# A recurrence and two MoE layers on one core: preparing chunks further ahead, solving two triangular systems together, and spreading the recurrence's steps between the MoE blocks

## The chip, the cores and the metric

The kernel runs on one core of one Trainium2 chip. The metric is the device time of one execution in microseconds (us). Engines are called as in the profile: PE is TensorE (matmuls), PEld its weight loads, DVE is VectorE, ACT is ScalarE, POOL is GpSimd, and SP is the engine that issues the DMAs here. A median over three runs is given, and one execution was recorded by the hardware profiler.

## What is computed

The reference is a recurrence over 768 time steps for 4 batches of 8 heads with a 40 by 40 state each, then a dense two-layer block (MoE1), then a mixture of 8 experts with dense gates (MoE2):

```python
# recurrence, for each t:  y_t = r_t S;  S <- S * w_t - (S a_t) b_t^T + v_t k_t^T
for t in range(S):
    y[:, :, t] = np.einsum('bhd,bhde->bhe', rt, state)
    Sa = np.einsum('bhde,bhe->bhd', state, at)
    state = state * wt[:, :, None, :] - np.einsum('bhd,bhe->bhde', Sa, bt) + np.einsum('bhd,bhe->bhde', vt, kt)
# MoE1, 3072 tokens, 320 -> 2048 -> 320
h = x @ w_in;  x = np.where(h > 0, h, np.exp(np.minimum(h, 0)) - 1) @ w_out
# MoE2: gates P normalised over rows and columns 8 times, then
for e in range(8):
    out += P[:, e:e + 1] * (np.maximum(x @ w1[e], 0) @ w2[e])     # 320 -> 1024 -> 320
```

## The kernel before

**Chunks.** The 768 steps are cut into 24 chunks of 32. Within a chunk the recurrence becomes matrix products and a triangular solve; from chunk to chunk the state Y is handed on. The work of one chunk c is cut into steps, each a small Python function:

- `ld` (lines 263 to 269) issues the DMAs of WA and KE; `lu` that of VU; `lv` those of rB and rO. WA, KE, xE, F and rO have one buffer each, VU three.
- `prep` (283 to 308) runs two scans on DVE (F, line 292, and xE, line 297) and element work on POOL (KE, line 306; aE, 299; WA, 307) and ACT. It needs WA and KE, and it ends with aE, its copy aB, and a scaled KE.
- `E3` (349) multiplies KE and aB on PE (line 338), masks the product on DVE into Am (line 342), writes Am to DRAM (Ad, line 357) and reads it back in another layout as LT (line 359). `E1` (313) and `E2` (322) transpose KE and xE on PE (lines 318, 328). `E4` multiplies Am by VU on PE (line 367).
- `T` is the solve (`tsolve_`, 370): a work tile Wk is loaded with a constant by DMA (line 374), then 31 rounds of two DVE instructions follow, a product (line 379, into Tt) and a subtraction (line 386, in Wk), each of which needs the one before it; Wk goes to DRAM (Td, line 390, four DMAs) and back as TT (line 394, four DMAs).
- `H1` (405; PE line 416) needs the state; `H2` (417; PE line 425) multiplies by TT; `H3` (435; PE line 446, DVE line 456) makes the new state Y; `H4` (458; PE line 465) transposes it into Ss.
- `O1` (473; PE line 479), `O2` (484; PE line 338, mask Gm on DVE line 342) and `O3` (488; PE lines 497 and 502, DVE line 504) make the chunk's output, which goes to DRAM as yd (line 509).

The recurrence proper is the ring H1, H2, H3 and H1 of the next chunk; E, T and prep of a chunk don't depend on the state and can be done ahead.

**MoE1.** Its 3072 tokens are 12 blocks of 256, two chunks each. A block begins with `xprep` (513): it reads two tiles yt (one buffer, line 520), transposes each on PE (line 523) into X by ACT (526) and DVE (527, 528). Then 16 units follow. A unit has two halves of eight 256-column matmuls: `m1_mm1` (534; PE line 538; g on DVE line 543, gh on ACT 545, gl on POOL 547) and, two units later, `m1_mm2` (552; PE lines 561 to 565), which reads gh and gl.

**What sets the order.** Instructions are traced in the order of the string PLAN["order"] (line 26), once per chunk: `m+2` stands for two halves of MoE1, `E3+2` for E3 of the chunk two ahead, `O1+-1` for O1 of the chunk before. On PE this order is kept literally in the loop (`pin`, line 115). On the other engines a list scheduler takes, by its own model of time, what is ready first, with the traced position as the priority (T and the MoE1 halves are put 300 places back, prep 300 forward, line 30); what it fixes is then the order in which the engine runs, strictly one after the other. PLAN["start"] (27) is a longer list for the first two chunks, in which MoE1's weights are also converted (`w`, 64-bit floats to pairs of 32-bit ones, with raw tiles from the pool cv, line 153). After the recurrence the rest of MoE1 and then MoE2 (lines 648 to 780) run on PE without a break.

Of the kernel before, what the change touches and what calls it, by code (L numbers as in the profile page):

```python
# [9 lines left out]
F32 = mybir.dt.float32  # L10
# [12 lines left out]
PLAN = {  # L23
# [74 lines left out]
def build(ctx, tc, r, k, v, w, a, b, w_in, w_out, wg, w1, w2, wa_d, kb_d, re_d, ro_d, vt_d, wp_d, consts, out, C, off):  # L98
    nc = tc.nc
# [50 lines left out]
    pa_p = moe.enter_context(tc.tile_pool(name="pa_p", bufs=1, space=PSUM))  # L150
    r1 = rec.enter_context(tc.tile_pool(name="r1", bufs=1, side="right"))
    r2 = rec.enter_context(tc.tile_pool(name="r2", bufs=2, side="right"))
    cv = cvx.enter_context(tc.tile_pool(name="cv", bufs=3, side="right"))
    rp = rec.enter_context(tc.tile_pool(name="rp", bufs=1, space=PSUM, side="right"))

    Wt = mw.tile([128, 5, DFF], F32R, name="Wt")
# [65 lines left out]
    first = {}  # L222
    Y = r1.tile([128, NG, B, D], F32, name="Y")
    Ss = r1.tile([128, NG, 2, 2, D], F32, name="Ss")
    TTs = [r1.tile([128, H, 64], F32, name=f"TT{i}") for i in range(3)]
    wr = r1.tile([128, 4 * NG, C + 1], F32, name="wr")
    wq = r1.tile([128, 4 * NG, C], F32, name="wq")
    dr = r1.tile([128, 4 * NG, C + 1], F32, name="dr")
    dq = r1.tile([128, 4 * NG, C], F32, name="dq")
    Yw = r1.tile([128, NG, B, 64], F32, name="Yw")  # L230
    Ywv = Yw[:, :, :, 0:D]
    Ams = [r1.tile([128, 2, H, 64], F32, name=f"Am{i}") for i in range(2)]
    Gm = r1.tile([128, 2, H, 64], F32, name="Gm")
    aB = r1.tile([128, NG, 2, 2, 64], F32, name="aB")
    rB = r1.tile([128, NG, 2, 2, 64], F32, name="rB")
    wmm = per.tile([128, NCH], F32, name="wmm")
    CI = C // 4

    work = {None: (wr, wq, dq, aB)}

    def rec_init():
        for t in (wr, wq, dr, dq):
            V.memset(t, 0.0)
        work[1] = (early(1, "wr", [4 * NG, C + 1]), early(1, "wq", [4 * NG, C]), early(1, "dq", [4 * NG, C]), early(1, "aB", [NG * 2 * 2, 64]).rearrange("p (g u j) t -> p g u j t", u=2, j=2))
        for t in work[1]:
# [37 lines left out]
    def prep(c):  # L283
        z = st[c]
        NX = 4 * NG
        wr, wq, dq, z.aB = work.get(c, work[None])
        wf = z.WA[0:HR, 0].rearrange("p g t -> p (g t)")
        wv = wf.rearrange("p (x t) -> p x t", x=NX)
        V.tensor_scalar(out=wr[0:HR, :, 1:C + 1], in0=wv[:, :, ::-1], scalar1=WLO, scalar2=WHI, op0=ALU.max, op1=ALU.min)
        V.tensor_scalar(out=wq[0:HR, :, 1:C], in0=wv[:, :, 0:C - 1], scalar1=WLO, scalar2=WHI, op0=ALU.max, op1=ALU.min)  # L290
        F = early(c, "F", [NX, C + 1])
        V.tensor_tensor_scan(out=flat(F)[0:HR], data0=flat(wr)[0:HR], data1=flat(dr)[0:HR], initial=0.0, op0=ALU.mult, op1=ALU.add)  # L292
        z.Wf = r2.tile([128, NX], F32, tag="Wf", name="Wf", bufs=3)
        G.tensor_copy(out=z.Wf[0:HR], in_=F[0:HR, :, C])
# [12 lines left out]
        G.tensor_tensor(out=wv, in0=wv, in1=wr[0:HR, :, 1:C + 1][:, :, ::-1], op=ALU.subtract)
        A.activation(out=wf, in_=wf, func=AF.Square, accum_out=wmm[0:HR, c:c + 1])
# [61 lines left out]
    def tsolve_(c):  # L370
        z = st[c]
        Wk = r2.tile([128, CI, C], F32, tag="Wk", name="Wk")
        tmp = r2.tile([128, CI * (C - 1)], F32, tag="Tt", name="Tt")
        SY.dma_start(out=Wk.rearrange("p i t -> p (i t)"), in_=consts[:, nidk:nidk + CI * C])
        for j in range(C - 1):
            ni = j // 4 + 1
            nt = C - 1 - j
# [13 lines left out]
        z.TT = TTs[c % 3]  # L391
# [93 lines left out]
        z = st[c]  # L485
        yield from masked(banks("O2", c)[0], 2 * D, lambda u, g: z.uE[:, u, g, :], rB, Gm)

    def O3(c):
        z = st[c]
        PO = banks("O3", c)  # L490
        x = z.xT
        y = x if c else mt.tile([128, 384], F32, tag="yt", name="yt", bufs=1)
        for j in range(2):
            if c > 0:
                for g in range(NG):
                    for bb in range(B):
                        pin(T.matmul(PO[j][C * bb:C * bb + C, D * g:D * g + D], lhsT=z.rO[64 * (bb % 2):64 * (bb % 2) + D, bb // 2, j, g, :], rhs=Ss[64 * (bb % 2):64 * (bb % 2) + D, g, bb // 2, j, :], start=(g == 0), stop=False, skip_group_check=True))
                        yield
# [446 lines left out]
    with ExitStack():  # L945
        loads(0)
        loads(1)
        SY.dma_start(out=cst, in_=consts[:, 0:ncst])
        SY.dma_start(out=wgs[:, 0:2, :], in_=wg[0:256, :].rearrange("(k p) e -> p k e", p=128))
        SY.dma_start(out=wgs[0:64, 2, :], in_=wg[256:320, :])  # L950

# [84 lines left out]
        for c in range(2, NCH + 1):  # L1036
            for n, o in order:
# [53 lines left out]
```

## Time and profile before

| | |
|---|---|
| median of 3 runs | 2436.05 us (2433.66 to 2437.01) |
| the profiled execution | 2433.81 us, its span 2431.9 us |
| PE busy | 2185.4 us, 90% of the span |
| PE weight loads | 1991.4 us, 82% |
| DVE | 1127.6 us, 46% |
| ACT | 731.1 us, 30% |
| POOL | 503.8 us, 21% |
| chain that ended last | PE 67%, DVE 19%, DMA 8% |

The profiled execution is 2.2 us below the median. Busy time of PE is what the profile models from the starts of pipelined matmuls; idle time "before" a group of instructions is that of its engine, with what ended it. Granted clock is the share of full speed (2.4 GHz) that TensorE had on average in a stretch; its other level is half of that, 1.2 GHz.

### The profile page before, as it was taken

To read this page: it belongs to the slowest core of one execution; us is meant where nothing else is said; L and a number is where in the kernel's file an instruction comes from. 1 tells how busy PE (TensorE), PEld (TensorE's weight loads), DVE (VectorE), ACT (ScalarE), POOL (GpSimd) and SP (SyncE) were. 2 spreads that over 40 slices of the span, in tenths; PEclk is the share of its full clock that TensorE was granted. 3 is DMA by queue.
4 is the path that set the end of the run, shared out by engine and by line. 5 is a ranking of instruction groups with operands and counts; after the bars stand their busy time and mean duration, and the time that the engine had idled before them with its cause. 6 is when DMAs were issued, how large, how long until landed. Compare 5 with 4: busy or idle time off the path is not lost.

```text
span 2431.9 us, 47949 instructions
## 1 busy us (share of the span) xinstructions
PE 2185.4 (90%) x19908; PEld 1991.4 (82%) x19908; DVE 1127.6 (46%) x2878; ACT 731.1 (30%) x1627; POOL 503.8 (21%) x570
## 2 busy tenths in 40 slices
PE   2557887888888889999999999999999999999998
PEld 2456776787877788889999999999999999999998
DVE  7898677777877764253222222222222222222222
ACT  2343443444444444532311211211211212212111
POOL 6353333333333322500200200200200101101000
PEclk9998898988899989999999999999999999999999
DMA  5342323333233321420100100100100100000000
GB/s 153 109 143 75 99 72 85 82 84 91 76 94 80 86 75 37 116 58 1 45 4 1 48 1 1 48 1 1 48 1 7 42 1 22 27 1 19 12 22 34
DMA packets 171771, 121.67 MB, mean 50 GB/s; under 512 B 103000, under 2 KB 151512, under 8 KB 171544
## 3 DMA queue, kind: packets, MB, share of 16 engines
q1 hardware_dynamic: 171544, 118.52, 17.9%
q8 instruction: 158, 2.59, 0.5%
q14 instruction: 69, 0.57, 0.1%
HBM read 99.99 MB, written 18.48 MB: 49 GB/s over the span
## 4 chain that ended last, share of the span: by engine, by line
PE 67%; DVE 19%; DMA 8%; issue 2%; SPq 2%; POOL 1%; ACT 1%; DVEq 0%; ACTq 0%; POOLq 0%
PE h L704 29%; PE pa L746 9%; PE pa L745 9%; PE pa L744 9%; DVE Wk L386 5%; DVE Tt L379 5%; PE ph L538 3%; DMA WA<-in_wa 2%; DMA LT<-Ad 1%; DVE g L543 1%; DMA yt<-yd 1%; DVE F L292 1%; DVE Gm L342 1%; DVE Am L342 1%; PE a L561 1%
## 5 line engine op out<-in xcount | busy, mean ns | idle before, releaser
L704 PE MATMUL h<-X,a 128*128 128x512 f32 x3072 | 774.8, 394 | 0.0
L708 DVE SCALAR_TENSOR_TENSOR hl<-h,hh 128x512 fp32r<-128x512 f32 x384 | 264.8, 690 | 879.7 <-ACT hh L707 879.4
L704 PEld LDWEIGHTS h<-X,a 128*128 128x128 f32 x3072 | 564.2, 188 | 102.9
L707 ACT ACTIVATE hh<-h 128x512 fp32r<-128x512 f32 x384 | 230.2, 600 | 1019.5 <-PE h L704 1015.9
L745 PE MATMUL pa<-a,hl 128*128 128x320 f32 x1536 | 474.5, 309 | 0.0
L744 PE MATMUL pa<-a,hh 128*128 128x320 f32 x1536 | 472.3, 309 | 1.1 <-ACT acc L751 0.9
L746 PE MATMUL pa<-a,hh 128*128 128x320 f32 x1536 | 468.7, 310 | 0.0
L745 PEld LDWEIGHTS pa<-a,hl 128*128 128x128 f32 x1536 | 288.8, 188 | 15.9
L744 PEld LDWEIGHTS pa<-a,hh 128*128 128x128 f32 x1536 | 288.8, 188 | 15.9 <-ACT acc L751 1.3
L746 PEld LDWEIGHTS pa<-a,hh 128*128 128x128 f32 x1536 | 287.3, 188 | 0.1
L672 POOL TENSOR_TENSOR a<-rw,a 128x384 fp32r<-128x384 f32 x64 | 65.6, 1025 | 1057.9 <-ACT a L670 1055.2
L538 PE MATMUL ph<-X,Wt 128*128 128x256 f32 x1536 | 252.2, 311 | 5.2 <-DVE g L543 5.1
L379 DVE TENSOR_TENSOR Tt<-Wk,LT 128x60 f32<-128x60 f32 (+24 forms) x744 | 209.0, 284 | 88.4 <-DMA LT<-Ad 59.2
L547 POOL TENSOR_TENSOR gl<-g,gh 128x256 fp32r<-128x256 f32 x192 | 159.1, 830 | 389.2 <-ACT gh L545 280.3
L538 PEld LDWEIGHTS ph<-X,Wt 128*128 128x128 f32 x1536 | 216.6, 209 | 14.3 <-DVE g L543 8.5
L386 DVE TENSOR_TENSOR Wk<-Wk,Tt 128x60 f32<-128x60 f32 (+24 forms) x744 | 215.2, 292 | 17.9
L545 ACT ACTIVATE gh<-g 128x256 fp32r<-128x256 f32 x192 | 80.0, 417 | 232.6 <-DVE g L543 190.0
L755 DVE SCALAR_TENSOR_TENSOR acc<-pa,Pg,acc 128x320 f32<-128x320 f32 x168 | 84.3, 544 | 114.8 <-PE pa L746 114.8
L543 DVE SCALAR_TENSOR_TENSOR g<-m,ph 128x256 f32<-128x256 f32 x192 | 79.9, 416 | 104.1 <-ACT m L541 95.3
L540 ACT ACTIVATE m<-ph 128x256 f32<-128x256 f32 x192 | 73.2, 381 | 89.7 <-PE ph L538 88.1
L541 ACT ACTIVATE m<-m 128x256 f32<-128x256 f32 x192 | 79.8, 416 | 4.7
L425 PE MATMUL P<-RH,TT 64*64 64x40 f32 x768 | 33.7, 248 | 48.7 <-DMA TT<-Td 47.1
(173 smaller groups left out, 2412.7 us busy)
## 6 DMA issues: line engine op xcount, KB each, us to landing
LT<-Ad SPq DMA_DIRECT2D x24, 512.0 KB
rw<-in_moe_w SPq DMA_DIRECT2D x64, 160.0 KB
WA<-in_wa SPq DMA_DIRECT2D x24, 416.0 KB
KE<-in_kb SPq DMA_DIRECT2D x24, 416.0 KB
rw<-in_moe_w SPq DMA_DIRECT2D x64, 128.0 KB
VU<-in_vt SPq DMA_DIRECT2D x24, 320.0 KB
raw<-in_wp SPq DMA_DIRECT2D x16, 384.0 KB
raw<-in_moe_w_out SPq DMA_DIRECT2D x16, 320.0 KB
```

The costliest lines, as they stand in the source:

```text
L379: V.tensor_tensor(out=tv, in0=Wk[:, 0:ni, j:j + 1].to_broadcast([128, ni, nt]), in1=z.LT[:, j, j + 1:C].unsqueeze(1).to_broadcast([128, ni ...
L386: dve["T"] = V.tensor_tensor(out=Wk[:, 0:ni, j + 1:C], in0=Wk[:, 0:ni, j + 1:C], in1=tv, op=ALU.subtract)
L538: pin(T.matmul(ph, lhsT=Wt[0:kp, wi, 128 * f:128 * f + 128], rhs=X[0:kp, xi, :], start=(i == 0), stop=(i == 7)))
L543: V.scalar_tensor_tensor(out=g, in0=m, scalar=-1.0, in1=ph, op0=ALU.add, op1=ALU.max)
L547: G.tensor_tensor(out=gl, in0=g, in1=gh.bitcast(F32), op=ALU.subtract)
L704: T.matmul(h, lhsT=a1[:, wi, :], rhs=X[bk][:, xi, :], start=(i == 0), stop=(i == 7))
L707: A.activation(out=hh, in_=h, func=AF.Relu)
L708: V.scalar_tensor_tensor(out=hl, in0=h, scalar=0.0, in1=hh.bitcast(F32), op0=ALU.max, op1=ALU.subtract)
L744: T.matmul(o, lhsT=hh[:, ts_], rhs=a2[:, 0, :], start=(f == 0), stop=False)
L745: T.matmul(o, lhsT=hl[:, ts_], rhs=a2[:, 0, :], start=False, stop=False)
L746: T.matmul(o, lhsT=hh[:, ts_], rhs=a2[:, 1, :], start=False, stop=(f == NF2 - 1))
L755: V.scalar_tensor_tensor(out=at, in0=o, scalar=Pg[:, tt, e:e + 1], in1=at, op0=ALU.mult, op1=ALU.add)
```

## The change

The loop's order and the start list are new, O3 is cut in two, T is called for two chunks at once, and buffers are added so that a chunk can be prepared three ahead (E3, E2, E1 for c+3; ld and prep for c+4, where it was E for c+2, prep for c+2 and ld for c+3). Wk is filled on POOL from a tile idk that is loaded once. To make room, cv has two buffers instead of three and a scratch area for DMA descriptors is smaller. The number of MoE1 halves per chunk (16 in the string) stays.

```diff
-    "order": "E4 H1 m+2 O1+-1 H2 m+3 O2+-1 H3 m+3 ld+3 lu+1 prep+2 O3+-1 m+2 H4 E3+2 T+2 m+2 E1+2 m+2 x E2+2 m+2 lv w",
+    "order": "E4 m+1 O2+-1 m+1 H1 x m+1 O3a+-1 m+1 lv H2 m+1 O3b+-1 m+2 H3 m+1 E3+3 m+2 H4 m+1 E2+3 m+1 E1+3 ld+4 lu+1 m+2 O1 prep+4 T+3 m+2 w",
     "start": ... O3_0 becomes O3a_0 O3b_0, O3_1 becomes O3a_1 O3b_1, and at its end
+     ... prep_4 E3_4 E2_4 E1_4 ld_5 prep_5
-    cv = cvx.enter_context(tc.tile_pool(name="cv", bufs=3, side="right"))
+    cv = cvx.enter_context(tc.tile_pool(name="cv", bufs=2, side="right"))
-    TTs = [... for i in range(3)]        # z.TT = TTs[c % 3]
+    TTs = [... for i in range(4)]        # z.TT = TTs[c % 4]
-    Ams = [... for i in range(2)]        # z.Am = Ams[c % 2]
+    Ams = [... for i in range(3)]        # z.Am = Ams[c % 3]
+    idk = r1.tile([128, CI * C], F32, name="idk")
     # Wf, KB, xT: 3 -> 4 buffers; aE: 2 -> 4
 def tsolve_(c):
-        SY.dma_start(out=Wk.rearrange("p i t -> p (i t)"), in_=consts[:, nidk:nidk + CI * C])
+        G.tensor_copy(out=Wk.rearrange("p i t -> p (i t)"), in_=idk)
-    def O3(c):
+    def O3a(c):       # the products of Ss and rO (line 497), for both j
+        if c == 0:
+            return
+    def O3b(c):       # the products of Gm and KB (line 502), the multiplication by xT, the store
     # in try_xprep
-            if ... and ("O3", 2 * xp + 1) in done:
+            if ... and ("O3b", 2 * xp + 1) in done:
     # in the loop over c
+                elif n == "T":
+                    if (c + o) % 2 and c + o < NCH:
+                        with tc.high_priority(offset=PLAN["po"]["T"]):
+                            tsolve(c + o - 1, c + o)
-    nc = bacc.Bacc("TRN2", target_bir_lowering=False, num_devices=1)
+    nc = bacc.Bacc("TRN2", target_bir_lowering=False, num_devices=1, dynamic_dma_scratch_size=4096)
```

`tsolve(c1, c2)` was there already, for the start list: it takes the rounds of the two solves alternately.

## Rows read from the trace of the kernel before

**Rows 1.** Busy time of the engines, granted clock and DMA in four stretches: start, steady recurrence, the rest of MoE1, MoE2.

```profile
core 0: us, PE busy (x) PEld busy (x) DVE busy (x) ACT busy (x) POOL busy (x), PEclk, DMA share, GB/s
0.00:250.00 250.00, 127.12 (x1945) 111.37 (x1945) 215.53 (x613) 87.46 (x205) 117.93 (x143) 0.94 0.43 120
250.00:950.00 700.00, 589.84 (x9449) 548.55 (x9450) 510.54 (x1551) 298.53 (x771) 240.79 (x265) 0.90 0.31 81
950.00:1100.00 150.00, 142.97 (x1168) 133.75 (x1167) 57.13 (x130) 72.70 (x164) 44.68 (x56) 0.98 0.27 78
1100.00:2431.00 1331.00, 1325.46 (x7349) 1197.70 (x7348) 344.45 (x584) 272.45 (x488) 100.43 (x106) 1.00 0.06 18
```

**Rows 2.** PE's waits in the steady stretch, 250 to 950 us: who waited for whom, us in total, times, the longest; and one group of PE instructions there, H4, which has 8 matmuls a chunk.

```profile
PE P L523 <- DMA yt<-yd: 40.2, 8, 5.7
PE a L562 <- POOL gl L547: 25.6, 8, 6.1
PE P L318 <- DVE Am L342: 16.3, 8, 2.1
PE P L523 <- DVE Tt L379: 8.6, 2, 4.8
PE P L338 <- DVE xT L504: 8.1, 7, 1.3
PE P L497 <- DVE Gm L342: 3.4, 7, 0.6
...
L465 PE MATMUL P<-cst,Yw 104*128 104x104 f32 x144 | 16.5, 259 | 0.0
```

**Rows 3.** DVE in the same stretch: the two instructions of the solve (busy, mean ns | idle before them), and DVE's waits.

```profile
L386 DVE TENSOR_TENSOR Wk<-Wk,Tt 128x60 f32<-128x60 f32 (+24 forms) x558 | 163.3, 293 | 15.3
L379 DVE TENSOR_TENSOR Tt<-Wk,LT 128x60 f32<-128x60 f32 (+24 forms) x558 | 160.5, 288 | 84.4 <-DMA LT<-Ad 59.2 <-DMA Wk<-in_consts 8.3 <-DMA Td<-Wk 2.0
...
DVE Tt L379 <- DMA LT<-Ad: 59.2, 14, 8.3
DVE g L543 <- ACT m L541: 50.0, 40, 4.8
DVE Am L342 <- PE P L338: 15.9, 9, 2.6
```

**Rows 4.** PE at full clock, from the timeline (start us, us, engine, line): H3, H1 and a half of MoE1.

```profile
655.74 1.30 PE L446 MATMUL P<-VU,KB 64*40 64x40 f32 x64
...
679.78 0.79 PE L416 MATMUL P<-Yw,aE 40*32 40x40 f32 x64
680.50 1.22 PE L538 MATMUL ph<-X,Wt 128*128 128x256 f32 x8
```

**Rows 5.** From the timeline (start us, us, engine, line): after an E1 the KE of the next chunk is fetched, POOL waits for it, and gl and a half of MoE1 behind it.

```profile
673.70 0.88 PE L318 MATMUL P<-cst,KE 104*128 104x104 f32 x8
...
675.63 0.43 SPq L269 DMA_DIRECT2D KE<-in_kb  x1
...
678.81 0.42 DVE L543 SCALAR_TENSOR_TENSOR g<-m,ph 128x256 f32<-128x256 f32 x1 [0.68 <-ACT m L541]
...
679.92 2.34 POOL L306 TENSOR_TENSOR KE<-KE,F 104x512 f32<-104x512 f32 x2 [4.10 <-DMA KE<-in_kb]
...
682.22 1.42 POOL L547 TENSOR_TENSOR gl<-g,gh 128x256 fp32r<-128x256 f32 x2
...
683.00 0.39 PE L562 MATMUL a<-gl,WoA 128*128 128x256 f32 x1 [1.15 <-POOL gl L547]
```

**Rows 6.** The timeline of one xprep: transposes of its first tile, the load of the second, its transposes, X; and a half of MoE1 just after it.

```profile
711.59 0.49 PE L523 MATMUL P<-cst,yt 128*128 128x128 f32 x3
...
713.64 0.60 SPq L520 DMA_DIRECT2D yt<-yd  x1
...
717.23 0.88 PE L523 MATMUL P<-cst,yt 128*128 128x128 f32 x3 [5.15 <-DMA yt<-yd]
...
718.14 0.49 ACT L526 ACTIVATE X<-P 128x384 fp32r<-128x384 f32 x1 [5.22 <-PE P L523]
718.49 2.06 PE L538 MATMUL ph<-X,Wt 128*128 128x256 f32 x8
...
719.97 0.40 DVE L527 TENSOR_TENSOR X<-P,X 128x256 fp32r<-128x256 f32 x1
720.29 0.28 DVE L528 TENSOR_TENSOR X<-P,X 128x128 fp32r<-128x128 f32 x1
```

**Rows 7.** DVE in the start list, where two solves run alternately (x2: two instructions together), and just after, where one of them has ended.

```profile
71.40 0.34 DVE L379 TENSOR_TENSOR Tt<-Wk,LT 128x28 f32<-128x28 f32 x2
71.66 0.34 DVE L386 TENSOR_TENSOR Wk<-Wk,Tt 128x28 f32<-128x28 f32 x2
71.92 0.34 DVE L379 TENSOR_TENSOR Tt<-Wk,LT 128x24 f32<-128x24 f32 x2
...
74.08 0.21 DVE L379 TENSOR_TENSOR Tt<-Wk,LT 128x48 f32<-128x48 f32 x1
74.32 0.21 DVE L386 TENSOR_TENSOR Wk<-Wk,Tt 128x48 f32<-128x48 f32 x1
74.56 0.21 DVE L379 TENSOR_TENSOR Tt<-Wk,LT 128x49 f32<-128x49 f32 x1
```

**Rows 8.** One solve from its first instruction to its last, its way to DRAM and back, and the H2 that needs it.

```profile
639.48 1.03 DVE L379 TENSOR_TENSOR Tt<-Wk,LT 128x31 f32<-128x31 f32 x1 [3.53 <-DMA LT<-Ad]
...
667.05 0.17 DVE L386 TENSOR_TENSOR Wk<-Wk,Tt 128x8 f32<-128x8 f32 x1
...
667.25 1.23 SPq L390 DMA_DIRECT2D Td<-Wk  x2
...
677.41 0.59 SPq L394 DMA_DIRECT2D TT<-Td  x1
...
684.90 0.31 PE L425 MATMUL P<-RH,TT 64*64 64x40 f32 x4
```

**Rows 9.** PE's longest wait in the start, 80 to 260 us.

```profile
PE P L425 <- DMA TT<-Td: 47.1, 8, 16.1
```

**Rows 10.** POOL: a copy of 64 columns and the difference gl of 256 (columns as on the page; the first from its line's own view: duration ns min/median/max).

```profile
L505 POOL COPY xT<-xT x23: 236/237/238, 130.9 to 980.2; 128x64 f32<-128x64 f32 x23
...
L547 POOL TENSOR_TENSOR gl<-g,gh 128x256 fp32r<-128x256 f32 x192 | 159.1, 830 | 389.2 <-ACT gh L545 280.3
```

More of the change, by code (lines that the diff above doesn't have):

```diff
@@ L224, in build @@
     Ss = r1.tile([128, NG, 2, 2, D], F32, name="Ss")
-    TTs = [r1.tile([128, H, 64], F32, name=f"TT{i}") for i in range(3)]
+    TTs = [r1.tile([128, H, 64], F32, name=f"TT{i}") for i in range(4)]
     wr = r1.tile([128, 4 * NG, C + 1], F32, name="wr")
@@ L231, in build @@
     Ywv = Yw[:, :, :, 0:D]
-    Ams = [r1.tile([128, 2, H, 64], F32, name=f"Am{i}") for i in range(2)]
+    Ams = [r1.tile([128, 2, H, 64], F32, name=f"Am{i}") for i in range(3)]
     Gm = r1.tile([128, 2, H, 64], F32, name="Gm")
@@ L249, in rec_init @@
             V.memset(bank[i], 0.0)
-        for t in (aB, wmm, rB, Ams[0], Ams[1], *TTs, Yw, Gm):
+        for t in (aB, wmm, rB, *Ams, *TTs, Yw, Gm):
             G.memset(t, 0.0)
@@ L292, in prep @@
         V.tensor_tensor_scan(out=flat(F)[0:HR], data0=flat(wr)[0:HR], data1=flat(dr)[0:HR], initial=0.0, op0=ALU.mult, op1=ALU.add)
-        z.Wf = r2.tile([128, NX], F32, tag="Wf", name="Wf", bufs=3)
+        z.Wf = r2.tile([128, NX], F32, tag="Wf", name="Wf", bufs=4)
         G.tensor_copy(out=z.Wf[0:HR], in_=F[0:HR, :, C])
@@ L297, in prep @@
         V.tensor_tensor_scan(out=flat(z.xE)[0:HR], data0=flat(wq)[0:HR], data1=flat(dq)[0:HR], initial=0.0, op0=ALU.mult, op1=ALU.add)
-        z.aE = r2.tile([128, NG, B * C], F32, tag="aE", name="aE")
+        z.aE = r2.tile([128, NG, B * C], F32, tag="aE", name="aE", bufs=4)
         G.tensor_tensor(out=z.aE[0:HR].rearrange("p g t -> p (g t)"), in0=z.WA[0:HR, 1].rearrange("p g t -> p (g t)"), in1=flat(z.xE)[0:HR], op=ALU.mult)
@@ L314, in E1 @@
         z = st[c]
-        z.KB = r2.tile([128, 2, H * D], F32, tag="KB", name="KB", bufs=3)
+        z.KB = r2.tile([128, 2, H * D], F32, tag="KB", name="KB", bufs=4)
         for u in range(2):
@@ L324, in E2 @@
         z = st[c]
-        z.xT = r2.tile([128, 384], F32, tag="xT", name="xT", bufs=3)
+        z.xT = r2.tile([128, 384], F32, tag="xT", name="xT", bufs=4)
         xv = z.xE.rearrange("p (g b) t -> p g (b t)", g=NG)
@@ L350, in E3 @@
         z = st[c]
-        z.Am = Ams[c % 2]
+        z.Am = Ams[c % 3]
         yield from masked(PS["E3"][0], HR, lambda u, g: z.KE[:, g, u, :], z.aB, z.Am)
@@ L390, in tsolve_ @@
             SY.dma_start(out=Td.rearrange("x (i q) t -> q x i t", q=4)[q], in_=Wk[q::4])
-        z.TT = TTs[c % 3]
+        z.TT = TTs[c % 4]
         for bb in range(B):
@@ L486, in O2 @@
         yield from masked(banks("O2", c)[0], 2 * D, lambda u, g: z.uE[:, u, g, :], rB, Gm)
-    def O3(c):
+    def O3a(c):
+        z = st[c]
+        PO = banks("O3", c)
+        if c == 0:
+            return
+        for j in range(2):
+            for g in range(NG):
+                for bb in range(B):
+                    pin(T.matmul(PO[j][C * bb:C * bb + C, D * g:D * g + D], lhsT=z.rO[64 * (bb % 2):64 * (bb % 2) + D, bb // 2, j, g, :], rhs=Ss[64 * (bb % 2):64 * (bb % 2) + D, g, bb // 2, j, :], start=(g == 0), stop=False, skip_group_check=True))
+                    yield
+    def O3b(c):
         z = st[c]
@@ L493, in O3 @@
         for j in range(2):
[L494 to L498, printed above, removed]
             for g in range(NG):
@@ L948, in build @@
         SY.dma_start(out=cst, in_=consts[:, 0:ncst])
+        SY.dma_start(out=idk, in_=consts[:, nidk:nidk + CI * C])
         SY.dma_start(out=wgs[:, 0:2, :], in_=wg[0:256, :].rearrange("(k p) e -> p k e", p=128))
@@ L958, in try_xprep @@
             xp = ms["xp"]
-            if (late or xp == 0) and xp < NB1 and xp <= bk + 1 and ("O3", 2 * xp + 1) in done:
+            if (late or xp == 0) and xp < NB1 and xp <= bk + 1 and ("O3b", 2 * xp + 1) in done:
                 xprep(xp)
@@ L990, in build @@
             wgen += wi_[k0 + i:k0 + i + 1] + wo_[i:i + 1]
-        fns = dict(ld=loads, lu=loadv, lv=loads2, prep=prep, H1=H1, H2=H2, H3=H3, H4=H4, E1=E1, E2=E2, E3=E3, E4=E4, T=tsolve, O1=O1, O2=O2, O3=O3,)
+        fns = dict(ld=loads, lu=loadv, lv=loads2, prep=prep, H1=H1, H2=H2, H3=H3, H4=H4, E1=E1, E2=E2, E3=E3, E4=E4, T=tsolve, O1=O1, O2=O2, O3a=O3a, O3b=O3b)
         done = {("ld", 0), ("ld", 1)}
```

2 rows, old and new, of the table PLAN are left out of this document.

## The prediction

> **What bounds the kernel now.** I read first the busy time by stretches. From 1100 us on PE is busy for all but 5.5 of 1331 us at full clock, and DVE, ACT and POOL have little to do: MoE2 is bound by PE, and the change doesn't touch it [rows 1]. The reader is to see in the same view that the stretch from 250 to 950 us is different: PE is busy for 590 of 700 us, at a granted clock of 0.90, so 110 us are idle and about 20% of the time (140 us) is at 1.2 GHz. Since PE's order is written out and all its work is the same before and after, the end moves by as much as idle time and half-clock time of PE change, wherever in the recurrence that is.
>
> 18 chunks pass in that stretch (144 transposes of H4, 8 a chunk [rows 2]), so a chunk takes 38.9 us. The second view is PE's waits there [rows 2]. Six waits make nearly all of the idle time: xprep's load of yt, 40.2 and 8.6 us (the second line names DVE's solve, but it stands before the same transposes, so I count it to yt: 48.8 us in 10 cases); gl from POOL, 25.6; E1 behind the mask of E3, 16.3; E3 behind the output's multiplication by xT, 8.1; O3 behind the mask Gm, 3.4. The third view is DVE [rows 1, 3]: it is busy for 510.5 us, of which the solve has 163.3 + 160.5 = 324, or 18.0 us a chunk, and it stands for 59.2 us before LT has landed.
>
> **Neighbours in PE's order.** Two waits come from steps that stand too near to each other. Before, E3 is followed by two halves of MoE1 and then E1, which overwrites a bank that E3's mask is still read from; O3 is followed by two halves and H4, and then E3, on a bank that O3's result is still read from. After, E3 and E1 have four halves, H4 and E2 between them; O3b and E3 three halves and H3. A half takes 1.22 us [rows 4], and these waits are at most 2.1 us long [rows 2], so one or two more halves are enough: 16.3 + 8.1, **minus 24 us** (0 at worst).
>
> A third pair comes nearer. The mask Gm is read from O2's bank, which O3's first products overwrite. Before, H3 and three halves stand between; after, H1 and two halves, 1.30 - 0.79 + 1.22 = 1.7 us less [rows 4]. In 7 of 18 chunks PE waited there already, 0.5 us each [rows 2]; x lies between in every second chunk after the change and hides it. That leaves 9 chunks: where it waited (3 or 4) 2.2 us, in the others something like 0.4, 10 us, against 3.4 before: **plus 7 us**, bounds -3 and 17.
>
> **gl.** KE has one buffer: when E1 (673.70) has read it, SP fetches the next at 675.63, POOL stands at KE's scaling until 679.92, takes 2.34 us for it, and only then makes two gl, while PE waits for the first until 683.00, 9.3 us after that E1 [rows 5]. After the change ld stands right behind E1 as well, so POOL will wait as long. But what PE does meanwhile is more: two halves, O1, two halves, E4, a half, O2, a half and H1, where it was four halves, E2, E4 and H1. Two added steps of about 1 us (E1 itself takes 0.88) cover most of a wait of 25.6/8 = 3.2 us in the mean. I take two thirds back: **minus 17 us**, with 0 and 25.6 as bounds.
>
> **xprep.** Its second yt can only be loaded when the first has been transposed, because yt has one buffer. The transposes begin at 711.59, the DMA is issued at 713.64, and the second set begins at 717.23, after 5.15 us of idling [rows 6]. The change leaves this as it is: the 48.8 us stay. But x moves. Before, two halves of the old block, or more, stand behind it; after, x stands between H1 and a single half. The first two halves traced at chunk 5 find no block prepared and are lost, so from there on each block's first m1_mm1 follows x at once, and has to wait for X. ACT's copy ends at 718.63 and DVE's last difference at 720.57, against 718.11 for the end of the transposes [rows 6]: 0.5 to 2.5 us for each of the 10 xpreps in the stretch. I take 1.3, which leaves out the scan that DVE ran in between: **plus 13 us**, bounds 5 and 25. The lost halves run later, where PE is dense, and cost nothing.
>
> **The clock.** Behind an idle xprep, a half of MoE1 takes 2.06 us [rows 6] instead of 1.22 [rows 4]. That slow piece will remain, since its idling remains. If the waits between near steps and for gl go, some of the others go with them; rows for a PE without them don't exist in this stretch. The bounds are 0 and 70 us (140 us at half rate cost at most half of that). I take a bit under a third, since xprep's share stays: **minus 20 us**.
>
> **The solve.** Two independent solves pack better: 71.40, 71.66, 71.92 are the starts of pairs, 0.26 us apart, while single rounds go every 0.24 us [rows 7]. Per pair of chunks that would save 62 x (2 x 0.24 - 0.26) = 13.6 us of DVE. I count nothing of it in the sum. The solves of a pair only run alternately if both are ready together, and the scheduler takes the first as soon as its LT is there (a solve begins where LT lands, 639.48 [rows 8]); their LT land a chunk apart. DVE also isn't what PE waits for most. The DMA of Wk goes, with 8.3 us of DVE's waits [rows 3]; the copy that replaces it costs POOL between 0.24 us (64 columns) and 0.83 (256 columns, two inputs) [rows 10], 6 to 20 us over 24 chunks, in the gaps in which POOL waits anyway. Where POOL runs just then, gl is late by that much, which the bound on gl holds.
>
> The Trainium skill, "VectorE: DVE Perf Modes", section "The DRAIN you can't avoid", speaks against the pairing: an operation starts only when the one before it has left the pipeline, so two alternating solves would cost as much as two in turn. Here the trace disagrees: two instructions in 0.26 us, not 0.48 [rows 7]. By the rule a pair would be 30 us of bare DVE time, by the rows 16.
>
> **The other buffers and the start.** More buffers of aE, Wf, KB, xT, Am and TT only take waits away. With two raw tiles the weights are converted more slowly, which gives DVE to the solves; prep and E of chunk 4 stand in the start, where DVE is busy for 215.5 of 250 us [rows 1]. PE's longest wait there is for TT, 47.1 us, up to 16.1 at a time [rows 9]. It could shrink, by at most 30 us, or grow by about one more solve, 18 us, since chunk 4's solve now shares DVE with chunk 5's. I take **0**. O3's split, the smaller scratch and the loads a chunk earlier move work without adding any: 0.
>
> **Sum.** 2433.8 - 24 + 7 - 17 + 13 - 20 = 2392.8 in the profiled execution's time; it is 2.2 us below the median of its runs, so 2395 us.
>
> **Rivals.**
>
> *The pairs come too late (slower).* Before, a solve ran for 27.6 us (639.48 to 667.22), because DVE does other work between its rounds, and H2 followed 17.7 us later, of which the way over DRAM, from 667.25 past the last issue at 677.41, takes some 12 [rows 8]. If the two solves of a pair do start together, at the end of an iteration, then H2 of the first is 1.3 iterations off, 51 us. At today's pace a pair takes 55 us, and 67 with the DMAs: 16 us late. At DVE's bare busy time it takes 36 + 12 = 48, in time. It decides at 39 us. Midway, 47 us, each of 10 pairs makes PE wait for 8 us: +80, less the 41 gained, 2475 us. For it speaks that TT is already the longest wait where DVE is full [rows 9]; against it, that the solve's data come a chunk earlier, and the 0.26 us [rows 7]. By the rule of the Trainium skill named above, a pair would keep its 36 us, which brings this case nearer; the trace is against the rule, as said there.
>
> *The waits only change places (no change).* gl's waits stay and the clock gives nothing back: 2433.8 - 24 + 7 + 13 = 2429.8, 2432 with the offset. DVE's queue speaks for it: 510.5 busy + 59.2 for LT + 50.0 for ACT + 15.9 for PE [rows 1, 3] are 635.6 us, 35.3 a chunk, so a chunk can't fall far below that while these waits stay, and a DVE that is nearly full makes g, and so gl, late. Against it, that PE has more to do in that time.
>
> *The pairs do pack (much faster).* DVE has 13.6/2 = 6.8 us less a chunk, and g, the masks and X come earlier: gl's waits go (-25.6), Gm's too (-3.4), X costs 5, the clock gives 50 and the start 20: 2433.8 - 24 - 25.6 - 3.4 + 5 - 50 - 20 = 2315.8, 2318 with the offset.
>
> *The pairing does nothing* is part of my forecast, as the solves may run one by one.
>
> **Chances.** Forecast 0.49 (its own range 2360 to 2425), late pairs 0.20, waits that change places 0.14, packed pairs 0.17. The range must leave out no more than 2 in 10: from 2305, below the packed case, to 2465, which leaves out a good half of the late pairs. Faster by over 0.2% (about the least that a measurement of this kernel tells from no change, 5 us): 0.49 + 0.17 and a little of the third case, 0.69. Within: 0.09. Slower: 0.22, the late pairs and what of the third case lies above.
>
> **What would show it.** In the trace of the changed kernel: no wait of E1 (line 318) for Am, nor of E3 for xT; gl's wait well below 25; about 5 us of idling at each xprep, and a further wait of the first half behind it for X; a wait of line 497 for Gm of about 10 us in all; a clock above 0.90 in the stretch; chunks of about 36.5 us; no wait of H2 for TT after the start. A wait of H2 for TT at every second chunk would prove the late pairs; alternating product instructions of two solves with 0.26 us between them, the packed ones. I am wrong if the half-clock share doesn't follow the idle time, or if the start grows.

## The result, and the profile after

The change makes the kernel slower: 2463.66 us (median of 4 runs, 2461.58 to 2467.37) against 2435.58 (4 runs, 2433.66 to 2437.01), a ratio of 1.0117 with a 95% interval of 1.0100 to 1.0135. The forecast was 41 us faster; it became 28 us slower.

Busy time, granted clock and DMA in the stretches of [rows 1] (columns as there):

```profile
0.00:250.00 250.00, 131.59 (x1936) 114.32 (x1938) 221.08 (x673) 85.92 (x201) 123.12 (x155) 0.90 0.44 121
250.00:950.00 700.00, 598.57 (x9204) 555.30 (x9199) 469.78 (x1481) 290.80 (x745) 214.06 (x271) 0.82 0.30 76
950.00:1100.00 150.00, 142.27 (x1277) 133.18 (x1275) 43.13 (x94) 75.86 (x177) 49.73 (x64) 0.92 0.27 74
1100.00:2459.00 1359.00, 1352.39 (x7502) 1222.80 (x7501) 363.08 (x633) 281.14 (x505) 100.32 (x106) 1.00 0.06 18
```

Set beside [rows 1], PE does wait less: up to 1100 us it is idle for 227.6 us instead of 240.1, and after 1100 us for 1 us more, some 11.5 us less in all. The span went from 2431.9 to 2459.7, 27.8 us more. So PE takes 39 us longer for the same 19908 matmuls. The clock column says why: in the steady stretch it fell from 0.90 to 0.82. Time at 1.2 GHz is twice what is missing from 1, so 140 us of the 700 became 252; over the first 1100 us, 176 became 326.

PE's waits in the steady stretch, all that are over 1 us:

```profile
PE P L530 <- DVE X L535: 51.1, 9, 10.1
PE P L497 <- DVE Gm L343: 19.0, 7, 4.4
PE a L569 <- POOL gl L554: 18.9, 10, 3.6
PE ph L545 <- DVE g L550: 5.4, 4, 2.0
PE ph L545 <- ACT X L533: 5.2, 9, 0.6
PE P L339 <- DVE uE L404: 1.6, 2, 0.8
```

Against [rows 2], E1's wait for Am and E3's for xT are gone, Gm's grew from 3.4 to 19.0, gl's fell from 25.6 to 18.9, and at xprep's transposes (line 530 now) the 48.8 became 51.1, with another releaser. No H2 waits for TT. VectorE's own waits show what changed at xprep:

```profile
DVE Tt L380 <- DMA LT<-Ad: 54.5, 17, 5.7
DVE xE L298 <- PE P L329: 39.7, 16, 4.5
DVE wr L290 <- DMA WA<-in_wa: 29.8, 11, 4.3
DVE g L550 <- ACT m L548: 26.4, 31, 3.9
```

prep of c+4 now stands close behind its own loads and behind E2 of c+3, and WA and xE have one buffer: VectorE stands for 29.8 us until WA has landed and 39.7 until PE has read xE. Whatever is behind prep in VectorE's fixed order waits too. One xprep, from the timeline of all engines:

```profile
671.01 0.90 PE L530 MATMUL P<-cst,yt 128*128 128x128 f32 x3
671.94 0.35 SPq L527 DMA_DIRECT2D yt<-yd  x1
...
673.10 1.38 DVE L343 TENSOR_TENSOR Gm<-P,cst 64x512 f32<-64x512 f32 x2
...
673.84 0.50 ACT L533 ACTIVATE X<-P 128x384 fp32r<-128x384 f32 x1
676.07 0.42 DVE L534 TENSOR_TENSOR X<-P,X 128x256 fp32r<-128x256 f32 x1
676.41 0.28 DVE L535 TENSOR_TENSOR X<-P,X 128x128 fp32r<-128x128 f32 x1
676.79 0.88 PE L530 MATMUL P<-cst,yt 128*128 128x128 f32 x3 [4.88 <-DVE X L535]
...
678.25 2.08 PE L545 MATMUL ph<-X,Wt 128*128 128x256 f32 x8 [0.58 <-ACT X L533]
680.25 1.29 PE L497 MATMUL P<-Ss,rO 40*32 40x40 f32 x64
681.48 0.58 PE L568 MATMUL a<-gh,WoB 128*128 128x256 f32 x1
...
683.48 1.87 PE L426 MATMUL P<-RH,TT 64*64 64x40 f32 x32
685.28 1.22 PE L545 MATMUL ph<-X,Wt 128*128 128x256 f32 x8
```

The second tile's transposes wait for a bank of PSUM, the memory that matmuls write, which VectorE reads late (676.07, more than 1.7 us after ACT has ended), not for yt alone. Behind the stop PE runs one half (2.08 us), O3a (1.29), one half, H2 (1.87), all at the low rate, and only at 685.28 does a half take 1.22 us again. The same in stretches: 17 us at half the clock, then full, then 10 us in which PE is busy throughout and the clock is half all the same.

```profile
650.00:668.00 18.00, 16.35 (x205) 15.56 (x205) 9.30 (x26) 8.15 (x20) 8.12 (x9) 1.00 0.50 119
668.00:685.00 17.00, 11.39 (x186) 9.77 (x187) 15.33 (x52) 4.61 (x13) 3.64 (x6) 0.50 0.13 34
685.00:709.00 24.00, 21.99 (x309) 21.05 (x308) 13.80 (x42) 12.45 (x31) 8.44 (x11) 1.00 0.46 119
709.00:719.00 10.00, 10.00 (x186) 9.02 (x185) 9.57 (x26) 3.81 (x12) 3.48 (x5) 0.50 0.09 20
```

In the trace's clock record of 250 to 950 us there are 16 pieces at 1.2 GHz, 15.8 us long in the mean, 14 of them over 10 us; before there were 26 of 5.6 us in the mean, 3 of them over 10 us. Behind the nine long stops at x (over 1.5 us) the low level lasts for 5.0 to 17.0 us from when PE goes on, 10.7 in the mean; before, behind ten, for 3.0 to 6.1, 4.5 in the mean.

### The profile page after: what moved, and what is told of

Its sections match the earlier page's. It is cut to its first block, busy times and chain, and to the rows that moved or that the text cites. A ratio compares the mean times of both kernels' runs of the same rounds, so it can differ in the third digit from the quotient of the medians.

```text
span 2459.7 us, 48041 instructions
## 1 busy us (share of the span) xinstructions
PE 2224.8 (90%) x19908; PEld 2025.6 (82%) x19908; DVE 1097.1 (45%) x2878; ACT 733.7 (30%) x1627; POOL 487.2 (20%) x596
## 4 chain that ended last, share of the span: by engine, by line
PE 72%; DVE 14%; DMA 8%; issue 2%; SPq 2%; ACT 1%; POOL 1%; DVEq 0%; ACTq 0%; POOLq 0%
PE h L711 29%; PE pa L753 9%; PE pa L752 9%; PE pa L751 9%; PE ph L545 5%; DMA WA<-in_wa 5%; DVE Tt L380 4%; DVE Wk L387 3%; PE a L568 2%; DVE F L293 1%; PE a L569 1%; PE a L570 1%; DVE Gm L343 1%; PE P L426 1%; PE P L509 1%
## 5 line engine op out<-in xcount | busy, mean ns | idle before, releaser
L752 PEld LDWEIGHTS pa<-a,hl 128*128 128x128 f32 x1536 | 288.9, 188 | 15.8
L545 PE MATMUL ph<-X,Wt 128*128 128x256 f32 x1536 | 258.9, 318 | 14.1 <-DVE g L550 6.7
L545 PEld LDWEIGHTS ph<-X,Wt 128*128 128x128 f32 x1536 | 224.1, 216 | 23.8 <-ACT X L533 10.5
L554 POOL TENSOR_TENSOR gl<-g,gh 128x256 fp32r<-128x256 f32 x192 | 143.6, 749 | 294.5 <-ACT gh L552 262.6
L387 DVE TENSOR_TENSOR Wk<-Wk,Tt 128x60 f32<-128x60 f32 (+24 forms) x744 | 184.9, 252 | 17.2
L569 PE MATMUL a<-gl,WoB 128*128 128x256 f32 x216 | 69.0, 319 | 16.6 <-POOL gl L554 16.6
```

The costliest lines, as they stand in the source:

```text
L387: dve["T"] = V.tensor_tensor(out=Wk[:, 0:ni, j + 1:C], in0=Wk[:, 0:ni, j + 1:C], in1=tv, op=ALU.subtract)
L545: pin(T.matmul(ph, lhsT=Wt[0:kp, wi, 128 * f:128 * f + 128], rhs=X[0:kp, xi, :], start=(i == 0), stop=(i == 7)))
L554: G.tensor_tensor(out=gl, in0=g, in1=gh.bitcast(F32), op=ALU.subtract)
L569: pin(T.matmul(o, lhsT=Wo(f)[:, 128 * i:128 * i + 128], rhs=gl, start=False, stop=False, skip_group_check=True))
L752: T.matmul(o, lhsT=hl[:, ts_], rhs=a2[:, 0, :], start=False, stop=False)
```

## The experiments

Each kernel was compared with the kernel before on the same chip (its medians there: 2437.1 to 2438.6 us). K is the granted clock of 250 to 950 us, "low" the time at 1.2 GHz in it, 1400 x (1 - K), and "idle" PE's idle time in it.

| kernel | us | ratio to before [95%] | idle | K | low |
|---|---|---|---|---|---|
| before | 2436 to 2439 | 1 | 110 | 0.90 | 140 |
| after | 2463.7 | 1.0117 [1.0100, 1.0135] | 101 | 0.82 | 252 |
| e1_x_back | 2473.3 | 1.0140 [1.0116, 1.0164] | 110 | 0.81 | 266 |
| e2_yt2 | 2472.2 | 1.0148 [1.0123, 1.0172] | 112 | 0.82 | 252 |
| e3_before_yt2 | 2396.4 | 0.9829 [0.9810, 0.9848] | 90 | 0.94 | 84 |
| e4_before_x | 2447.2 | 1.0036 [1.0024, 1.0047] | 119 | 0.88 | 168 |
| e5_single_T | 2464.5 | 1.0105 [1.0088, 1.0122] | 106 | 0.81 | 266 |
| e6_grouped | 2409.8 | 0.9884 [0.9862, 0.9906] | 103 | 0.89 | 154 |
| e7_before_spread | 2454.6 | 1.0064 [1.0047, 1.0081] | 104 | 0.86 | 196 |
| e8_grouped_yt2 | 2380.9 | 0.9765 [0.9748, 0.9781] | 84 | 0.92 | 112 |
| e9_ld_early | 2471.2 | 1.0144 [1.0116, 1.0171] | 109 | 0.82 | 252 |
| e10_group_at_stops | 2416.6 | 0.9911 [0.9889, 0.9934] | 127 | 0.90 | 140 |
| e11_group_elsewhere | 2520.3 | 1.0322 [1.0294, 1.0350] | 128 | 0.79 | 294 |

### The place of x and the buffer of yt

The first four runs asked whether x, which now stands between H1 and a single half, is the loss.

**e1_x_back**: the changed kernel, x behind H4.

```diff
-... H1 x m+1 O3a+-1 ... H4 m+1 E2+3 ...
+... H1 m+1 O3a+-1 ... H4 m+1 x E2+3 ...
```

> The changed kernel with one word moved: x (xprep) stands between H4 and E2+3, where the block that is running still has halves left, instead of between H1 and O3a. Theory A, the place of x is the loss: its idling (7.2 us a block in the changed kernel, 5.1 before) falls into the stretch where single halves alternate with small steps, and the clock stays low for 10 to 24 us behind it. Then this kernel is faster than the one before, 2400 to 2430 us, with a granted clock of 0.88 or more between 250 and 950 us. Theory B, the spreading into single halves costs the clock by itself, wherever x stands: 2450 to 2465 us and a clock of 0.82 to 0.84.

**e2_yt2**: the changed kernel with two yt buffers (and less descriptor scratch, to make room).

```diff
-yt = mt.tile([128, 384], F32, tag="yt", name="yt", bufs=1)
+yt = mt.tile([128, 384], F32, tag="yt", name="yt", bufs=2)
```

> The changed kernel with two buffers for yt (and a DMA scratch of 2048 bytes to make room), x where the change put it: the second tile of a block is there when the first has been transposed, so most of the idling at x goes (51 us of waits between 250 and 950 us). Theory A with the idling as the trigger of the low clock: idle time and the low stretch behind it go together, 2375 to 2400 us, clock 0.90 or more. Theory B: the idling goes but the clock stays near 0.83, 2410 to 2425 us.

**e3_before_yt2**: the kernel before with the same two buffers (and less scratch too).

> The kernel before with two buffers for yt (and the smaller DMA scratch of the change to make room), nothing else of the change: what the wait for yt costs there, 48.8 us of idling between 250 and 950 us and the slow halves behind it. Theory A: 2435.6 - 49 - about 10 to 20 of clock = 2365 to 2380 us. Theory B says nothing of this kernel beyond the idling: 2385 us. If another wait takes its place: 2400 us or more.

**e4_before_x**: the kernel before with x right behind H1.

```diff
-E4 H1 m+2 O1+-1 ... E1+2 m+2 x E2+2 ...
+E4 H1 x m+2 O1+-1 ... E1+2 m+2 E2+2 ...
```

> The kernel before with only x moved, from between E1 and E2 to behind H1, so that each block's first half follows its xprep at once, as in the changed kernel. Theory A: slower than before by most of the change's loss and of the gain that it hides, 2450 to 2475 us, with a clock below 0.87 between 250 and 950 us. Theory B: the order is as dense as before, 2436 to 2448 us, the wait for X alone (about 10 us).

Putting x back didn't help (2473.3), and putting it into the new place in the kernel before cost 9 us (a ratio of 1.0036), a third of the loss at most. So the place of x isn't the main cause. Of the four, only e4_before_x came out as a theory had it (B); e1_x_back and e2_yt2 are slower than either theory said, and e3_before_yt2 lies between theory B's 2385 us and the 2400 of a wait that takes the place of yt's.

e1_x_back is no clean test of x alone, since its wait for Gm in front of O3a grew from 19.0 to 44.5 us (16 times):

```profile
PE P L497 <- DVE Gm L343: 44.5, 16, 4.1
```

Its trace shows something else, within one kernel. Behind its nine stops at x, of 3.2 to 7.0 us, the low level lasts for 3.2 to 5.9 us; there E2's four transposes, a half, E1's eight transposes and another half follow. Behind the fourteen stops of over 1.5 us in front of O3a, most of them shorter (1.5 to 4.1 us), it lasts for 4.8 to 13.5 us, 10.3 in the mean; there O3a's 64 small matmuls, a half, H2, a half and O3b follow. One stop of either kind:

```profile
674.00:682.00 8.00, 3.63 (x20) 3.66 (x21) 3.60 (x12) 1.34 (x3) 0.76 (x2) 0.57 0.46 120
682.00:698.00 16.00, 11.98 (x197) 10.74 (x195) 14.61 (x36) 7.38 (x20) 7.51 (x9) 1.00 0.33 86
698.00:709.00 11.00, 10.92 (x155) 10.23 (x156) 7.51 (x34) 4.41 (x11) 1.01 (x3) 0.53 0.22 69
```

So neither the stop's length nor single halves as such go with a long low time; this points to what PE runs right behind the stop.

The second buffer is worth 41 us in the kernel before, more than any part of the change was meant to give, and nothing in the changed one. The trace of e2_yt2 shows why: the second transposes still stop for 6.67 us, though no load is waited for; the profile names no releaser, but they go on 0.1 us after VectorE has taken X from the bank, which it begins 1.74 us after ACT has ended (all engines, in order of time).

```profile
674.66 0.50 ACT L533 ACTIVATE X<-P 128x384 fp32r<-128x384 f32 x1
676.90 0.42 DVE L534 TENSOR_TENSOR X<-P,X 128x256 fp32r<-128x256 f32 x1
677.24 0.28 DVE L535 TENSOR_TENSOR X<-P,X 128x128 fp32r<-128x128 f32 x1
...
677.62 0.87 PE L530 MATMUL P<-cst,yt 128*128 128x128 f32 x3 [6.67 <-issue]
```

In the kernel before, the buffer takes PE's idle time from 110 to 90 us and the low time from 140 to 84.

### Spreading against late VectorE

**e6_grouped**: the changed kernel, look-ahead, buffers and pairs kept, the 16 halves in groups of two and three.

```diff
-E4 m+1 O2+-1 m+1 H1 x m+1 O3a+-1 m+1 lv H2 m+1 O3b+-1 m+2 H3 m+1 E3+3 m+2 H4 m+1 E2+3 m+1 E1+3 ld+4 lu+1 m+2 O1 prep+4 T+3 m+2 w
+E4 H1 m+2 O2+-1 H2 m+3 O3a+-1 O3b+-1 lv H3 m+3 E3+3 m+2 H4 m+2 x E2+3 m+2 E1+3 ld+4 lu+1 m+2 O1 prep+4 T+3 w
```

> The changed kernel with its look-ahead (E and prep three and four ahead) and its pair of solves, but with the MoE1 halves standing in groups of two and three between the recurrence steps, as the kernel before has them. Two theories are left of why the granted clock is lower after the change. Theory S (spreading): each stop of TensorE brings the clock to the 1.2 GHz level as before, but single halves between the recurrence's small matmuls keep it there longer (pieces of 10 to 24 us in the changed kernel against 3.4 to 10 us before). Theory D (VectorE is late): the stops themselves are the cause, since the loads of a chunk are now issued just ahead of prep and VectorE waits for them (wr<-WA 29.8 us), with X, Gm and g queued behind. S expects pieces of 3 to 10 us, a granted clock of 0.88 or more in 250:950 and 2415 to 2440 us. D expects the stops and pieces of the changed kernel, a clock of 0.82 to 0.85 and 2450 to 2470 us.

**e7_before_spread**: the counterpart, the kernel before with its 16 halves spread.

```diff
-E4 H1 m+2 O1+-1 H2 m+3 O2+-1 H3 m+3 ld+3 lu+1 prep+2 O3+-1 m+2 H4 E3+2 T+2 m+2 E1+2 m+2 x E2+2 m+2 lv w
+E4 m+1 H1 m+1 O1+-1 m+1 H2 m+2 O2+-1 m+1 H3 m+2 ld+3 lu+1 prep+2 O3+-1 m+1 H4 m+1 E3+2 T+2 m+2 E1+2 m+2 x m+1 E2+2 m+1 lv w
```

> The kernel before with its look-ahead and its order of steps, but with the MoE1 halves put singly or in twos between all steps (as many in a chunk, x after as many halves as before). S expects longer pieces at the 1.2 GHz level (more than 200 us of it in 250:950 against some 140 before), a clock of 0.85 or less there, and 2450 to 2475 us. D expects loads a chunk ahead of prep, as before, so the clock of before within 0.02 and 2428 to 2445 us.

**e9_ld_early**: the changed kernel, `ld+4` at the head of the order.

> The changed kernel with the loads of chunk c+4 issued at the head of chunk c's steps and not just ahead of prep. D expects VectorE's wait wr<-WA to fall from 29.8 us to under 8 in 250:950, TensorE's waits on X (51) and Gm (19) to fall by half, a clock of 0.88 or more and 2420 to 2445 us. S expects the wait on the loads to go as well, TensorE to gain no more than 10 to 15 us by it, the pieces at 1.2 GHz to stay at 10 to 24 us each, a clock of 0.85 or less and 2445 to 2462 us.

**e5_single_T**: the changed kernel without the pairing of solves.

> The changed kernel with each chunk's triangular solve called by itself instead of for two chunks together. All theories expect no difference, since in the trace of the changed kernel the two solves of a call run one after the other: 2457 to 2470 us and a clock of 0.81 to 0.84 in 250:950. If the pairing held VectorE up, it would be 2435 to 2450 us with less waiting on X and Gm.

First the steady stretch of e6_grouped, then that of e7_before_spread:

```profile
250.00:950.00 700.00, 597.27 (x9715) 565.00 (x9714) 482.04 (x1516) 308.41 (x794) 222.98 (x284) 0.89 0.29 76
```

```profile
250.00:950.00 700.00, 595.51 (x9218) 557.05 (x9219) 500.34 (x1523) 288.96 (x746) 212.98 (x258) 0.86 0.32 80
```

e6_grouped tells the two theories apart: PE is idle for 102.7 us, as in the changed kernel (101.4), but the low time is 154 us instead of 252, and the kernel is 54 us faster than the changed one and 1.2% faster than before, a little faster than S said. Against e1_x_back, where x also stands between H4 and E2, it is 63 us faster. Its stops are no shorter; PE's waits at x, two lines with different releasers, come to 54.3 us:

```profile
PE P L530 <- DMA yt<-yd: 33.1, 6, 7.1
PE P L530 <- DVE Tt L380: 21.2, 3, 7.2
```

What is different is how long the clock stays down: pieces of 7.5 us in the mean, against 15.8. e7_before_spread shows part of this from the other side: 6 us less idle time than before, 56 us more at 1.2 GHz, 0.6% slower, so the spreading costs clock there too. But it contradicts S in how: its pieces are not longer, they are more, 34 of 5.8 us in the mean against 26 of 5.6, and behind its stops at x, where a half, E2 and another half follow, the low level lasts for 2.7 to 5.9 us, no longer than before. It goes only part of the way to the changed kernel: 196 us low at K 0.86, just short of the 200 and 0.85 that S expected, with the time inside its range. Its start ran at a clock of 0.71 (0.94 before); in e3_before_yt2 it was 0.71 too, and that kernel is faster than before. What lowers it there stayed open, but it costs nothing: PE is busy for 126 to 128 us of these 250 us in all three. The kernel before itself varies like that: over the whole execution its clock was 0.931 to 0.938 in five of the seven executions beside these runs and 0.959 and 0.961 in two, at 2436 to 2442 us either way.

e9_ld_early didn't take away the wait that it was made for (wr for WA: 31.9 us, was 29.8), since WA has a single buffer: POOL's product aE (line 300) still read it at 620.7 us, and the DMA was issued at 622.5, against 621.7 and 623.0 in the changed kernel. So it says nothing of what that wait costs. e5_single_T is the changed kernel again (2464.5 us), as expected: the pairing makes no difference.

### What PE does right behind a stop

e6_grouped also moved steps. The last pair of runs only moved halves within the changed order.

**e10_group_at_stops**: three halves together behind x, three behind O3a.

```diff
-E4 m+1 O2+-1 m+1 H1 x m+1 O3a+-1 m+1 lv H2 m+1 O3b+-1 m+2 H3 m+1 E3+3 m+2 H4 m+1 E2+3 ...
+E4 m+1 O2+-1 H1 x m+3 O3a+-1 m+3 lv H2 O3b+-1 m+1 H3 m+1 E3+3 m+1 H4 m+1 E2+3 ...
```

> The changed kernel with three halves together right behind x and three together right behind O3's first part (the two places where TensorE stops once in a pair of chunks), and single halves elsewhere. Theory S, made sharper: what TensorE does right behind a stop sets how long it stays at 1.2 GHz. It expects pieces of 3 to 10 us, less than 190 us of them in 250:950 (after 253), a clock of 0.86 or more and 2410 to 2435 us. If it is the spreading over the whole chunk that counts, wherever the stop is, the clock stays at 0.82 to 0.85 and the time at 2445 to 2465 us.

**e11_group_elsewhere**: single halves there, groups of three and four later in the chunk.

```diff
-... O3b+-1 m+2 H3 m+1 E3+3 m+2 H4 m+1 E2+3 m+1 E1+3 ld+4 lu+1 m+2 O1 prep+4 T+3 m+2 w
+... O3b+-1 m+1 H3 E3+3 m+4 H4 E2+3 E1+3 ld+4 lu+1 m+3 O1 prep+4 T+3 m+3 w
```

> The counterpart: single halves behind x and behind O3's first part as in the changed kernel, and groups of three and four in the second half of a chunk's steps, where TensorE hardly stops. The sharper S expects pieces of 10 to 24 us as in the changed kernel, a clock of 0.81 to 0.85 in 250:950 and 2445 to 2470 us. If grouping anywhere is enough, the clock is 0.87 or more and the time 2410 to 2435 us.

**e8_grouped_yt2**: e6_grouped with two yt buffers.

> The changed kernel with the MoE1 halves in groups and a second yt buffer, so that both tiles of a block can be fetched at once. Grouping alone gave 2409.8 us with 54 us of TensorE's waiting at the transposes of x (33 for yt, 21 for X behind VectorE's solve). If that waiting is free to go, the part for yt (33 us) goes, and with it some pieces at 1.2 GHz: 2365 to 2390 us. If VectorE's queue sets it as in the changed order with two buffers, the wait is renamed and the time stays at 2400 to 2415 us.

The steady stretch of e10_group_at_stops, its two longest waits, and one stop at x with the stretches around it:

```profile
250.00:950.00 700.00, 573.04 (x9532) 537.24 (x9529) 471.72 (x1506) 299.34 (x777) 233.14 (x280) 0.90 0.30 76
```

```profile
PE P L530 <- DVE X L535: 70.2, 9, 9.9
PE P L497 <- DVE Gm L343: 29.0, 8, 3.8
```

```profile
616.00:643.00 27.00, 21.82 (x406) 20.32 (x405) 19.33 (x62) 13.26 (x35) 11.90 (x15) 1.00 0.35 90
643.00:653.00 10.00, 5.64 (x25) 5.26 (x26) 8.45 (x31) 1.71 (x4) 0.82 (x2) 0.50 0.11 31
653.00:687.00 34.00, 29.93 (x524) 28.06 (x523) 22.50 (x66) 16.09 (x42) 13.15 (x16) 1.00 0.38 96
```

This kernel waits *more* than the changed one, 127 us against 101 (X 70.2, Gm 29.0), and is 47 us faster (2416.6). So the late VectorE alone is not what makes the changed kernel slow, and the clock's time does not follow the idle time. Behind its stops at x the low level lasts for 4.3 to 7.7 us, 6.0 in the mean, and behind those in front of O3a for 3.5 to 6.4. Of its low time much is spent standing still, where the clock costs nothing: laying the clock record over the instructions, PE is busy at 1.2 GHz for 114 us of the first 1100, in the changed kernel for 249, before for 143.

e11_group_elsewhere is slower still, 2520.3 us, K 0.79, out of the range of either theory. Groups elsewhere don't help. Its longest piece at 1.2 GHz is 37.5 us:

```profile
690.00:700.00 10.00, 6.62 (x59) 6.22 (x57) 3.90 (x11) 5.26 (x13) 4.14 (x3) 1.00 0.56 143
700.00:738.00 38.00, 33.65 (x431) 30.29 (x432) 26.61 (x78) 10.45 (x26) 9.85 (x12) 0.51 0.22 57
738.00:752.00 14.00, 11.53 (x97) 11.04 (x95) 8.72 (x18) 7.44 (x19) 6.33 (x6) 0.98 0.41 111
```

PE is busy for 33.65 of those 38 us, with a half of MoE1 and a step of the recurrence in turn; its only stop of over 1 us behind 701 us is one of 2.5. The piece ends within the second of four halves in a row. This kernel has a second loss, a wait of 73 us for g where four halves stand together, so its time is not a price for the spreading alone. Nor is its clock, since all three pieces of 37.5 us begin at a stop for g.

e8_grouped_yt2 is the fastest kernel here: 2380.9 us, 2.3% faster than before. Grouped, the second buffer does give its gain (29 us on e6_grouped); what PE still waits for is VectorE and ACT:

```profile
PE ph L545 <- DVE g L550: 24.0, 22, 1.9
PE P L319 <- DVE X L535: 23.8, 6, 4.4
PE P L530 <- ACT gh L552: 17.8, 10, 4.5
```

## Why the prediction was wrong, step by step

- **The clock: the step that failed.** The prediction gave it -20 us, with "The bounds are 0 and 70 us", because "If the waits between near steps and for gl go, some of the others go with them". Those waits did go or shrink, and the idle time fell by 11.5 us, and the clock's part was +39 instead. No bound had the sign of a loss, since I took the clock for a function of idle time. The runs show another thing: with the same idle time (101 and 103 us) it is 0.82 or 0.89 by the order of the steps and halves, and with more (127), the halves alone moved, 0.90. Behind a stop, two or more halves in a row brought the full clock back within some 4 to 8 us; with halves one at a time between steps of 32 or 64 small matmuls (64x40, 40x40) it took 10 to 17 us in five of nine cases at x, although PE was busy. The prediction named this as what would make it wrong, "if the half-clock share doesn't follow the idle time". What about those small matmuls keeps the clock down was not measured.

  The Trainium skill, "TensorE: Matmul & The Clock Gate", section "Terms", reckons the cost of the lower clock as half the time spent at it. The traces agree in part, and only if the time in which PE is busy is counted: the changed kernel against e6_grouped, 249 - 163 = 86 us less, half of it 43, and 3 us less idle time make 46; the spans differ by 49. From the kernel before to the changed one the same reckoning gives too much: 249 - 143 = 106 us more, half of it 53, and PE was busy for 39 us more. Counted with the standing time, e10_group_at_stops would gain nothing on the kernel before or lose by it; by the busy time it would gain 10 us, and it gained 20.

- **Neighbours: right.** -24 us, measured 16.3 + 8.1 us, both waits gone.
- **Gm: right in kind, too small.** +7 us, measured +15.6, near the upper bound of 17. Its longest wait is 4.4 us, longer than two halves and H1 explain: VectorE makes the mask late. In one case PE had done O2 at 387.8 us, and the mask began at 392.79, behind prep's scan F (1.25 us) and rounds of the solve.
- **gl: too large.** -17 us, measured -6.7, inside its bounds.
- **xprep: right in sum, wrong in cause.** 48.8 + 13 = 61.8 us forecast; measured 51.1 + 5.2 = 56.3. The first half's wait for X is 5.2 (the lower bound). The stop itself is no longer yt's: e2_yt2 took yt's part away and the stop stayed. The step's "leaves this as it is" overlooked that VectorE's queue would become late: `prep+4` stands behind `E2+3` and `ld+4` with single buffers of xE and WA, 69.5 us of waiting there, where VectorE's waits before had 7.3 for xE and none over 2 us for WA. "The loads a chunk earlier move work without adding any" was wrong for the same reason: measured against prep, they come later. The place in the string is not all of it: in e6_grouped, with the same look-ahead, these two waits come to 7.7 + 6.1 = 13.8 us.
- **Solve: right.** Pairs ran one by one, no H2 waited for TT, and e5_single_T took the pairing away for no difference. So neither the late pairs nor the packed ones came about, and the changed kernel can't test the rule on alternating instructions that was weighed there. The section of the Trainium skill that the prediction cites for it also says that a next operation that is not held starts earlier, so it speaks less against the pairing than the prediction had it.
- **Start: right in sum.** 0 us, measured 4.5 us less idle and 4.5 us more busy. PE's longest wait there shrank by 31 us against [rows 9], and others took its place, at 80 to 260 us of the changed kernel:

```profile
PE P L426 <- DMA TT<-Td: 16.1, 3, 8.8
PE P L497 <- DVE Gm L343: 12.8, 2, 8.1
PE P L319 <- ACT xT L404: 11.5, 2, 6.2
PE P L339 <- POOL KE L307: 5.9, 1, 5.9
```

The terms for idle time in the steady stretch sum to -24.4 + 15.6 - 6.7 + 7.5 = -8.0 us, and the stretch shows -8.7, so nothing of size is missing among them: forecast was -21. With the clock, 59 us off, this is the whole difference between -41 and +28, to about 2 us. The look-ahead itself was no loss: with the halves grouped it is in e6_grouped, 29 us faster than before; with two yt buffers in both, e8_grouped_yt2 is some 15 us faster than e3_before_yt2.

## What to carry to other kernels

Where filler matmuls share TensorE with many small ones, try runs of two or three right behind the places where TensorE stops, and not one at a time for evenness: the order of the same work was worth 47 us here with the halves alone moved, more than all the waits that the change removed. Judge such a change by the granted clock as well as by the idle time, and give the clock's term both signs. Before deepening a look-ahead, look whether the loads and single buffers keep their distance from the step that reads them, since a wait in one in-order queue makes everything behind it late; what that was worth by itself no run here shows.

## What was not expected of the hardware

TensorE stayed at 1.2 GHz while it was working nearly without a break: 33.65 of 38 us in e11_group_elsewhere, 10.00 of 10 us in the changed kernel at 709 us, where the stop ahead of it was 2.0 us, 10.92 of 11 us in e1_x_back at 698 us. The lower level slows the small matmuls nearly as much as the large: O3's first part takes 1.29 us instead of 0.79, H2 1.87 instead of 1.13, a half 2.08 instead of 1.22. And the second yt buffer, which the prediction had not looked for, was worth 41 us in the median. Its profiled execution, the slowest of four, is 33 us shorter than that of the kernel before: in the steady stretch PE stood still for 20 us less, and was busy at the low clock for 87 us instead of 118, half of which is 16.
